# RWKV-7 attention and a quick-GELU MLP in one kernel: where the 64-bit words of the fifth weight piece are staged

## The chip, the cores and the metric

The kernel runs on one core of a Trainium2 chip. The metric is the device time of one execution, in microseconds (us); lower is better. A core has a matrix engine (PE, also called TensorE; its weight loads are listed as PEld), a vector engine (DVE), a scalar engine (ACT), a general engine (POOL), and a queue engine (SP) that issues the DMAs. Each of them takes its instructions strictly in the order in which the program lists them.

## The reference, cut to what matters

```python
def _attn_ref(r, k, v, w, a, b):            # each [4, 8, 768, 40]
    state = np.zeros((B, H, D, D), dtype=np.float32)
    for t in range(S):
        y[:, :, t] = np.einsum('bhd,bhde->bhe', rt, state)
        Sa = np.einsum('bhde,bhe->bhd', state, at)
        state_decay = state * wt[:, :, None, :] - np.einsum('bhd,bhe->bhde', Sa, bt)
        state = state_decay + np.einsum('bhd,bhe->bhde', vt, kt)
    return y

def _moe_ref(x, w_in, w_out):               # x [3072, 320]
    h = x @ w_in                            # w_in [320, 2048]
    g = h * (1.0 / (1.0 + np.exp(-1.702 * h)))
    return g @ w_out                        # w_out [2048, 320]
```

The y of the attention, with its heads laid side by side, is the x of the MLP. The two weight matrices come as 64-bit floats; everything else is 32-bit.

## The kernel before, in words

The sequence of 768 steps is cut into 12 *chunks* of 64. A *unit* is one chunk for two of the four batches, so there are 24 units, numbered i = 2c + p for chunk c and half p. Within a unit the recurrence is turned into matrix products. `decay` makes running products of w; `prep` scales a, b and k by them and forms score matrices; `inverse` inverts a triangular matrix by five doubling levels (the `ps_level` products), in a plain form for the first four units (`PLAIN = 4`, with the tile `PT`) and in another form after them; `solve` applies the inverse (`ps_X`), forms y and the new state (`ps_y`), and writes x, the transposed y. x goes out to DRAM (`part_with`, L911) and comes back in the layout that the MLP needs (`get_back`, L915), into the tile `xT`, of which there are three copies, one for each of three consecutive chunks. Each unit fills one half of its chunk's copy.

`mlp(c)` then does chunk c: products `ps_up` with `w_in`, the activation on ACT (L936), products `ps_down` with `w_out`, and the output store (L959). The down product runs over p and over eight parts m; part m = 0, 1 needs the first piece of `w_out`, 2, 3 the second, and so on.

The weights are loaded once, in eight pieces: 0 to 3 are `w_in`, 4 to 7 are `w_out`. A piece is 1280 64-bit numbers per partition, 1.31 MB. [...]`weight(n, ...)` loads the raw words somewhere (L436), and five steps make 32-bit floats of them in their final place in the tile `w_sb`: L416 on ACT, and L420, L424 and L425, L428 and L432 on DVE. The raw words of a piece take the space of two finished pieces. They lie in one of the following places:

- a half of the tile `extra`, which has room for two pieces of words; this document calls the halves a and b;
- a place inside `w_sb` that a later piece will fill. Piece 1 lies in the place of pieces 4 and 5, piece 2 in that of 6 and 7.

`before` lists the earlier pieces whose words lay at the same spot; the DMA waits until they are finished. `there` lists the pieces whose words still lie where this piece's result goes; L416 waits for those. So pieces 4 and 5 can't be converted before piece 1 is finished, and 6 and 7 not before piece 2. In the kernel before, the list of spots is

```python
raws = [-4, 4, 6, -2, -4, -2, -4, -2]       # -4: half a of extra, -2: half b, 4 and 6: in w_sb
```

The order of all work is made by `Plan`. Every step is a task with a rank, a set of engines that may do it with their assumed durations, and what it reads and writes. `order` simulates the engines: when one comes free, it takes the ready task of lowest rank. `paced` repeats this a few times and spreads the MLP's tasks of a chunk over the time until the next chunk is ready. The instructions are then issued in that order, and each engine waits in it, for its semaphores, at run time. The pieces' ranks are 14, 16, 20, 24, 35, 37, 39, 41; unit i has ranks around 10 i, so piece 4 stands between the work of units 3 and 4. The MLP has ranks from 10000, so it fills whatever the units leave free.

Of the kernel before, what the change touches and what calls it, by code (L numbers as in the profile page):

```python
# [21 lines left out]
INT64 = mybir.dt.int64  # L22
# [203 lines left out]
def rwkv7_gelu_quick(ctx: ExitStack, tc: tile.TileContext, time_d, v_d, w_d, wc_d, ak_d, b_d, rv_d, w_in, w_out, out):  # L226
    nc = tc.nc
    H, D, S = 8, 40, out.shape[0] // 4
    DM = H * D
# [3 lines left out]
    PIECE = w_in.shape[2]  # L233
    NF = w_in.shape[0] * PIECE // DM
    NM = NF // 2
    NK = DM // 64
# [18 lines left out]
    plan = Plan(dict(logw=3, wc=3, G=1, wch=3, wz=2, time=2, ak=2, b=2, rv=2, FT=3, GT=1, kh=2, bh=2, zr=2, rz=2,  # L255
                     A=1, B=1, RV=2, E0=2, W0=2, P21=2, PT=2, W=2, E=2, ES=2, EX=2, T=2, Tc=1, QT=1, zraw=2, zT=1, M=2, x=1, xT=3, g=4, ob=1), 4)
    tiles, psums, drams = {}, {}, {}

    def single(name, shape):
        return const.tile(shape, FP32, tag=name, name=name)  # L260

    def buf(name, n, shape, dt=FP32):

        if (name, n) not in tiles:
            s = n % plan.slots[name]
            tiles[name, n] = work.tile(shape, dt, tag=f"{name}{s}", name=name)
        return tiles[name, n]
# [20 lines left out]
    def act(n):  # L288
        return {"ACT": 210.0 + 0.76 * n}
# [39 lines left out]
    for p in HALF:  # L329
        q = slice(p.start, p.start + MID)  # L330
# [61 lines left out]
    w_sb = single("w_sb", [128, NK * NM * 128 + NF * DM])  # L392
    w_in_sb = w_sb[:, :NK * NM * 128].rearrange("p (m k f) -> p m k f", m=NM, k=NK)
    w_out_sb = w_sb[:, NK * NM * 128:]

    extra = single("extra", [128, 4 * PIECE])


    most, least = (float(np.array(x, np.uint32).view(np.float32)) for x in (0x0FEFFFFF, 0x9FEFFFFF))


    raws = [-4, 4, 6, -2, -4, -2, -4, -2]

    def weight(n, rank, src):
        at = raws[n]
        raw = lambda: (w_sb[:, at * PIECE:(at + 2) * PIECE] if at > 0 else extra[:, (at + 4) * PIECE:(at + 6) * PIECE]).bitcast(INT64)

        scale = lambda: w_sb[:, n * PIECE:(n + 1) * PIECE].bitcast(INT32)

        before = [("weight", m) for m in range(n) if raws[m] == at]  # L410
        there = [("weight", m) for m in range(n) if raws[m] in (n, n - 1)]
        word = lambda dt, w: raw().bitcast(dt).rearrange("p (n two) -> p n two", two=2)[:, :, w]

        def rebased(t):

            nc.scalar.activation(scale().bitcast(FP32), word(FP32, 1), ACT.Prelu, scale=2.0 ** -112, alpha=2.0 ** 32)  # L416

        def bounded(t):

            nc.vector.tensor_scalar(scale().bitcast(FP32), scale().bitcast(FP32), least, most, ALU.max, ALU.min)  # L420

        def exponent(t):

            nc.vector.tensor_scalar(word(INT32, 1), scale(), 3, -2 ** 23, ALU.logical_shift_left, ALU.bitwise_and)  # L424
            nc.vector.tensor_single_scalar(scale(), scale(), 3, op=ALU.logical_shift_left)  # L425

        def fraction(t):
            nc.vector.scalar_tensor_tensor(word(FP32, 1), in0=word(UINT32, 0), scalar=2.0 ** -52, in1=word(FP32, 1),  # L428
                                           op0=ALU.mult, op1=ALU.mult)

        def joined(t):
            nc.vector.tensor_add(scale().bitcast(FP32), scale().bitcast(FP32), word(FP32, 1))  # L432

        one, two = 170.0 + 0.48 * PIECE, 150.0 + 1.05 * PIECE
        T = lambda *names: [(name, n) for name in names]
        plan.add(rank, {"SP": 350.0}, lambda t: nc.sync.dma_start(raw(), src), reads=before, writes=T("wt"), size=128 * PIECE * 8)  # L436
        plan.add(rank, act(PIECE), rebased, reads=T("wt") + there, writes=T("rebased"))
        plan.add(rank, {"DVE": one, "sbuf": True}, bounded, reads=T("rebased"), writes=T("bounded"))
        plan.add(rank, {"DVE": 2 * one, "sbuf": True}, exponent, reads=T("bounded"), writes=T("exponent"))
        plan.add(rank, {"DVE": two, "sbuf": True}, fraction, reads=T("exponent"), writes=T("fraction"))  # L440
        plan.add(rank, {"DVE": two, "sbuf": True}, joined, reads=T("fraction"), writes=T("weight"))

    def weights():
        for n in range(len(raws)):
            weight(n, RANKS[n], w_in[n] if n < NQ else w_out[n - NQ])
# [116 lines left out]
    at = lambda tiles, n: tiles[n % len(tiles)]  # L562
# [1 line left out]
    both = lambda i: zr_of(i)[:, :8 * 104].rearrange("p (j n) -> p j n", n=104)  # L564
    zraw_of = lambda i: buf("zraw", i, [128, 8, D])
    M_of = lambda i: buf("M", i, [128, 8, 104])
    xT_of = lambda c: buf("xT", c, [128, 2, NK, 128])
    kh_of, bh_of = lambda i: kh_t[i % 2], lambda i: bh_t[i % 2]
    zT_of = lambda i: zT_t[i % plan.slots["zT"]]

# [216 lines left out]
    def solve(i):  # L787
        c, p = divmod(i, 2)
        R = 20 * (i // 2) + 5 * (i % 2)
        T = lambda *names: [(n, i) for n in names]  # L790
        ahT = lambda: ak_of(i)[:, 0]

        if c > 0:
            plan.add(R, {"DVE": 490.0, "sbuf": True}, lambda t: nc.vector.tensor_mul(
                both(i)[:, :, 64:], zraw_of(i - 2), wz_of(i).unsqueeze(2).to_broadcast([128, 8, D])),
                     reads=[("zraw", i - 2), ("wz", i)], writes=T("zr"))
# [12 lines left out]
            def read_state(t):  # L809

                ps, rT = psum(t, "ps_rz"), rv_of(i)[:, 0]
                for u, b in product(BITS, BITS):
                    for f, e in QUARTERS:
# [5 lines left out]
                     reads=T("zT"), writes=T("rz"), pair=("rz", i))  # L819
# [94 lines left out]
            for h in HALF:  # L914
                nc.sync.dma_start(xT_of(c)[h, p].rearrange("q k n -> q (k n)"), drams[i].rearrange("(q k) n -> q (k n)", q=64))  # L915
        plan.add(-50, {"SP": 700.0}, part_with, reads=T("x"), writes=T("xd"), size=DM * 512)
        plan.add(-50, {"SP": 700.0}, get_back, reads=T("xd"), writes=[("xT", c), ("xs", (c, p))], size=2 * DM * 512)


    g_of = lambda n: buf("g", n, [128, 2, 2, 256])  # L920
# [60 lines left out]
    for i in range(NU):  # L981
        decay(i)
        if i + 3 < NU:
            load_w(i + 3)
        if i + 2 < NU:
            logarithm(i + 2)
        if i >= 2:
            load(i)
        prep(i)
        inverse(i)  # L990
        solve(i)
        if i % 2:
            mlp(i // 2)
# [88 lines left out]
```

## Time and profile before

| | us |
|---|---|
| median of 3 runs | 727.67 (726.9 to 730.33) |
| the profiled execution's own time | 732.38 |
| its span, first to last instruction | 730.7 |
| PE busy in the span | 679.2 (93%) |
| PEld busy | 557.8 (76%) |
| DVE busy | 426.6 (58%) |
| ACT busy | 352.8 (48%) |
| POOL busy | 211.1 (29%) |

The profile is of one execution, and the times of single instructions come from it. Busy times of engines overlap. The strip shows the busy share of 40 equal slices of the span in tenths; a row of a timeline gives start, duration, engine, source line, operation and tiles, and in brackets how long the engine stood idle before it and what released it. All matrix products have the line L275, so they are told apart by their tiles. Rows with SPq are DMAs being issued; the transfer itself goes on afterwards.

### The profile page before, as it was taken

Reading aid. Unit: us, or ns where it says so; the run is one execution under the profiler, and the core shown is the slowest. Engines: PE = TensorE matmul, PEld = TensorE weight load, DVE = VectorE, ACT = ScalarE, POOL = GpSimd, SP = SyncE. Lnnn points to the kernel's source line nnn. Section 1 sums busy time; section 2 is a strip of 40 time slices with the busy share of each in tenths; the row PEclk is TensorE's granted clock in tenths of the full one; section 3 lists DMA queues with packets and bytes.
Section 4 is the critical chain, followed back from the end, with each engine's and each line's share of the span. In section 5 each row is a group of like instructions: output and inputs, shape, how many; then the busy total and the mean of one; then the engine's idle time right before and its main releaser. Section 6 shows DMA issues by size and latency. Waiting matters only on the chain.

```text
span 730.7 us, 43534 instructions
## 1 busy us (share of the span) xinstructions
PE 679.2 (93%) x20256; PEld 557.8 (76%) x20256; DVE 426.6 (58%) x747; ACT 352.8 (48%) x672; POOL 211.1 (29%) x281
## 2 busy tenths in 40 slices
PE   4575998998999999999999999999999999999997
PEld 4565876686778788888878888879889778867564
DVE  6569798965665656656664655647566666431000
ACT  4465755557445745535636444544536345341120
POOL 7015133522322532333431441331342431200000
PEclk9869999999999999999999999999999999999999
DMA  7952553431422441331340341331341230111000
GB/s 220 346 177 85 173 179 117 123 108 44 127 76 73 118 125 41 117 103 57 100 139 28 104 140 40 109 100 58 100 120 38 79 93 6 40 48 31 15 6 20
DMA packets 31860, 69.81 MB, mean 96 GB/s; under 512 B 5056, under 2 KB 14272, under 8 KB 30656
## 3 DMA queue, kind: packets, MB, share of 16 engines
q1 hardware_dynamic: 31680, 67.03, 29.9%
q8 instruction: 159, 2.61, 1.4%
q14 instruction: 21, 0.17, 0.1%
HBM read 59.15 MB, written 7.86 MB: 92 GB/s over the span
## 4 chain that ended last, share of the span: by engine, by line
PE 83%; DVE 5%; issue 4%; ACT 4%; POOL 2%; DMA 2%; SPq 0%; POOLq 0%; ACTq 0%; DVEq 0%
PE ps_down L275 27%; PE ps_up L275 27%; PE ps_level L275 8%; PE ps_B L275 5%; PE ps_y L275 4%; PE ps_X L275 3%; PE ps_Q L275 2%; PE ps_T L275 1%; PE ps_rz L275 1%; PE ps_A L275 1%; PE ps_N L275 1%; PE ps_zT L275 1%; PE ps_RV L275 1%; DVE w_sb L432 1%; DMA rv<-in_rv 1%
## 5 line engine op out<-in xcount | busy, mean ns | idle before, releaser
L275 PE MATMUL ps_up<-xT,w_sb 64*64 64x256 f32 x3840 | 256.5, 380 | 4.6 <-issue 3.2
L275 PE MATMUL ps_down<-w_sb,g 64*64 64x320 f32 x3072 | 240.1, 431 | 2.4 <-DVE w_sb L432 1.9
L275 PEld LDWEIGHTS ps_up<-xT,w_sb 64*64 64x64 f32 x3840 | 160.4, 134 | 33.9 <-issue 6.7
L275 PEld LDWEIGHTS ps_down<-w_sb,g 64*64 64x64 f32 x3072 | 126.6, 133 | 49.3 <-DVE w_sb L432 2.2
L936 ACT ACTIVATE g<-ps_up 128x1024 f32<-128x1024 f32 x48 | 49.2, 1024 | 48.8 <-PE ps_up L275 48.6
L585 POOL TENSOR_TENSOR kh<-time,G 128x320 f32<-128x320 f32 x24 | 21.8, 909 | 168.1 <-PE ps_y L275 89.9
L664 ACT ACTIVATE EX<-ES,quads 128x256 f32<-128x256 f32 x102 | 46.2, 501 | 47.3 <-DVE ES L659 46.9
L275 PEld LDWEIGHTS ps_level<-W,EX 64*64 64x64 f32 x2560 | 57.0, 134 | 11.2 <-issue 2.3
L708 ACT COPY W<-ps_level 128x512 f32<-128x512 f32 x56 | 32.8, 585 | 60.0 <-PE ps_level L275 58.3
L839 ACT COPY B<-ps_B 128x416 f32<-128x416 f32 x44 | 22.3, 506 | 73.1 <-PE ps_B L275 73.1
L275 PE MATMUL ps_level<-W,EX 64*64 64x64 f32 (+1 forms) x2560 | 56.9, 219 | 0.5 <-ACT EX L664 0.4
L710 DVE TENSOR_TENSOR E<-two,ps_level 128x256 f32<-128x256 f32 x80 | 33.3, 416 | 40.3 <-ACT W L708 39.9
L275 PE MATMUL ps_level<-PT,EX 64*64 64x64 f32 (+2 forms) x1280 | 35.5, 246 | 14.5 <-DVE EX L680 6.8
L275 PEld LDWEIGHTS ps_level<-PT,EX 64*64 64x64 f32 x1280 | 32.8, 146 | 20.6 <-issue 9.4
L962 DVE TENSOR_TENSOR ob<-ob,ps_down 128x320 f32<-128x320 f32 x24 | 11.7, 487 | 62.9 <-ACT ob L960 62.6
L901 POOL TENSOR_TENSOR x<-zr,FT 128x128 f32<-128x128 f32 x84 | 44.4, 557 | 0.4 <-POOL bh L585 0.4
L659 DVE STREAM_TRANSPOSE ES<-E 128x256 f32<-128x256 f32 x80 | 35.6, 445 | 4.3
L275 PE MATMUL ps_y<-RV,kh 64*64 64x104 f32 x768 | 36.0, 250 | 0.9 <-DVE M L855 0.9
L275 PE MATMUL ps_y<-M,bh 64*64 64x104 f32 x768 | 36.1, 249 | 0.2 <-issue 0.2
L577 POOL TENSOR_TENSOR ak<-ak,FT 128x512 f32<-128x512 f32 x22 | 28.6, 1299 | 26.5 <-ACT FT L539 9.7
L855 DVE TENSOR_TENSOR M<-ps_X,later 128x832 f32<-128x832 f32 x24 | 24.6, 1023 | 19.8 <-PE ps_X L275 19.8
L666 POOL TENSOR_TENSOR EX<-ES,quads 128x512 f32<-128x512 f32 x19 | 26.7, 1404 | 23.6 <-DVE ES L659 16.7
(138 smaller groups left out, 1144.4 us busy)
## 6 DMA issues: line engine op xcount, KB each, us to landing
ak<-in_ak SPq DMA_DIRECT2D x48, 160.0 KB
time<-in_time SPq DMA_DIRECT2D x24, 320.0 KB
rv<-in_rv SPq DMA_DIRECT2D x48, 160.0 KB
xT<-x_dram SPq DMA_DIRECT2D x48, 160.0 KB
wc<-in_wc SPq DMA_DIRECT2D x20, 264.0 KB
extra<-in_w_out SPq DMA_DIRECT2D x4, 1280.0 KB
logw<-in_w SPq DMA_DIRECT2D x24, 160.0 KB
b<-in_b SPq DMA_DIRECT2D x48, 80.0 KB
```

The costliest lines, as they stand in the source:

```text
L275: nc.tensor.matmul(o, lhsT, rhs, start=start, stop=True, skip_group_check=True)
L577: plan.add(R, {"DVE": 690.0, "POOL": 1270.0, "sbuf": True}, lambda t: of(t.engine).tensor_mul(ahT(), ahT(), FT_of(i)), reads=T("ak", "FT") ...
L585: plan.add(R + 4, {"POOL": 870.0, "DVE": 490.0, "sbuf": True}, lambda t, n=n, dst=dst: of(t.engine).tensor_mul(dst(i)[:, :, :D], by_head(t ...
L659: plan.add(rank, dve(256), lambda t: nc.vector.transpose(ES(n), source(t)), writes=[key("ES", n, 6)], **reads)
L664: nc.scalar.activation(dst[:, :, h], ES(n), ACT.Copy, scale=quads[:, h, :1])
L666: of(t.engine).tensor_mul(dst, ES(n).unsqueeze(2).to_broadcast([128, 8, 2, 32]), quads.unsqueeze(1).to_broadcast([128, 8, 2, 32]))
L708: plan.add(rank, any2(512), lambda t: copy(t.engine)(tiles_of(W(n + 1)), blocks(psum(t, ""), 64)), writes=[key("W", n + 1, 5)], pair=pair)
L710: plan.add(rank, dve(256), lambda t: nc.vector.tensor_sub(tiles_of(E(n + 1)), every(two32, [128, 2, 4, 32]), blocks(psum(t, ""), 64)[:, :, ...
L839: plan.add(R, any2(416), lambda t: copy(t.engine)(dst(), psum(t, "")[:, :, :208]), writes=[("Bv", i)] if x and c > 0 else T("B"), pair=(na ...
L855: plan.add(R + 1, dve(832), lambda t: nc.vector.tensor_tensor(M_of(i).rearrange("p (j b) n -> p b j n", b=2), psum(t, "")[:, :, :416].rear ...
L901: of(t.engine).tensor_mul(x[:, b ^ u, b], both(i)[:, at, :64], FT_of(i)[:, at])
L936: plan.add(-45, act(1024), lambda t: nc.scalar.activation(g_of(c * NQ + q).rearrange("p m r n -> p r m n"), psum(t, "").rearrange("p r (m ...
```

## The change

The raw words of piece 4 no longer lie in half a of `extra`. They lie in the second and third copy of `xT`, which are together exactly as large as the words of one piece. For that, the three copies of `xT` become one tile, `xT_all`, of the same total size. The pieces after the fifth change halves: 5 and 7 lie in a, 6 in b. The x of chunks 1 and 2, the first to use those two copies, is fetched back only once piece 4 is finished. Ranks, costs and the conversion steps are as before; `PLAIN` is 4 in both kernels.

| piece | 0 | 1 | 2 | 3 | 4 | 5 | 6 | 7 |
|---|---|---|---|---|---|---|---|---|
| words before | a | w_sb 4, 5 | w_sb 6, 7 | b | a | b | a | b |
| DMA waits for piece | - | - | - | - | 0 | 3 | 4 (and 0) | 5 (and 3) |
| words after | a | w_sb 4, 5 | w_sb 6, 7 | b | xT 1, 2 | a | b | a |
| DMA waits for piece | - | - | - | - | - | 0 | 3 | 5 (and 0) |

```diff
     extra = single("extra", [128, 4 * PIECE])
+    xT_all = single("xT_all", [128, plan.slots["xT"], 2 * NK * 128])
...
-    raws = [-4, 4, 6, -2, -4, -2, -4, -2]
+    spots = {"a": (extra, 0), "b": (extra, 2), "w4": (w_sb, 4), "w6": (w_sb, 6)}
+    raws = ["a", "w4", "w6", "b", "x", "a", "b", "a"]
 
     def weight(n, rank, src):
         at = raws[n]
-        raw = lambda: (w_sb[:, at * PIECE:(at + 2) * PIECE] if at > 0 else extra[:, (at + 4) * PIECE:(at + 6) * PIECE]).bitcast(INT64)
+        def raw():
+            if at == "x":
+                return xT_all[:, 1:].rearrange("p s n -> p (s n)").bitcast(INT64)
+            tile, k = spots[at]
+            return tile[:, k * PIECE:(k + 2) * PIECE].bitcast(INT64)
...
         before = [("weight", m) for m in range(n) if raws[m] == at]
-        there = [("weight", m) for m in range(n) if raws[m] in (n, n - 1)]
+        there = [("weight", m) for m in range(n) if raws[m] in (f"w{n}", f"w{n - 1}")]
...
-    xT_of = lambda c: buf("xT", c, [128, 2, NK, 128])
+    xT_of = lambda c: xT_all[:, c % 3].rearrange("p (q k n) -> p q k n", q=2, n=128)
...
-        plan.add(-50, {"SP": 700.0}, get_back, reads=T("xd"), writes=[("xT", c), ("xs", (c, p))], size=2 * DM * 512)
+        plan.add(-50, {"SP": 700.0}, get_back, reads=T("xd") + ([("weight", raws.index("x"))] if c in (1, 2) else []), writes=[("xT", c), ("xs", (c, p))], size=2 * DM * 512)
```

## The prediction

> **What bounds the kernel now.** The strip of 40 slices comes first, to find the stage that a change in weight loading can touch.
>
> ```profile
> PE   4575998998999999999999999999999999999997
> DMA  7952553431422441331340341331341230111000
> ```
>
> Each digit is 18.3 us. After the tenth slice TensorE is full, and nothing that is ready sooner can help it there; all that can be won is in the first ten slices. I then cut those at the events around the weights (busy time per engine by stage):
>
> ```profile
> 20.00:50.00 30.00, 17.99 (x492) 16.46 (x493) 18.49 (x24) 15.46 (x31) 1.47 (x2) 0.68 0.84 294
> 50.00:75.00 25.00, 15.85 (x708) 14.34 (x700) 22.80 (x31) 14.18 (x37) 11.41 (x11) 0.97 0.25 76
> 80.60:107.60 27.00, 25.55 (x770) 23.49 (x766) 21.42 (x28) 17.50 (x26) 7.78 (x8) 1.00 0.48 164
> 107.60:131.70 24.10, 19.27 (x689) 16.59 (x682) 21.83 (x29) 14.21 (x28) 9.34 (x7) 0.93 0.37 123
> 180.00:730.70 550.70, 540.42 (x15836) 438.43 (x15827) 290.35 (x550) 252.20 (x470) 148.41 (x183) 1.00 0.26 75
> ```
>
> The columns are window, length, busy PE, PEld, DVE, ACT, POOL, clock, DMA share, GB/s. PE idles 4.83 us in 107.6 to 131.7, and its clock is below full; it idles 10.3 us in the whole 550 us after 180. In 50 to 75 DVE is the bound (22.8 of 25.0); in 20 to 50 none is, and the DMA engines are at 0.84. What ends the idle time of 107.6 to 131.7 is in PE's timeline (start, length, idle before, releaser):
>
> ```profile
> 114.17 1.31 PE L275 MATMUL ps_down<-w_sb,g 64*64 64x320 f32 x16 [0.56 <-DVE w_sb L432]
> ...
> 121.66 0.69 PE L275 MATMUL ps_level<-PT,EX 64*64 64x64 f32 x32 [0.49 <-POOL EX L666]
> 123.60 1.66 PE L275 MATMUL ps_X<-B,T 64*64 64x104 f32 x32 [1.24 <-DVE T L781]
> 125.05 0.91 PE L275 MATMUL ps_B<-RV,A 64*64 64x104 f32 x16
> ...
> 131.69 1.31 PE L275 MATMUL ps_down<-w_sb,g 64*64 64x320 f32 x16 [1.35 <-DVE w_sb L432]
> ```
>
> Two parts of the first down product wait for L432, the last step of converting a weight piece. Between the down parts of 116.45 and 131.69 there is no MLP work, so PE is left with the short steps of units 3 and 4, whose gaps stay open. Why the last piece (number 7) is that late is in the timelines of SP, ACT and DVE:
>
> ```profile
> 77.90 0.33 SPq L436 DMA_DIRECT2D extra<-in_w_out  x1
> ```
>
> ```profile
> 103.98 1.46 ACT L416 ACTIVATE w_sb<-extra 128x1280 f32<-128x1280 f32 x1 [1.82 <-DMA extra<-in_w_out]
> 113.91 1.42 ACT L416 ACTIVATE w_sb<-extra 128x1280 f32<-128x1280 f32 x1 [0.49 <-DMA extra<-in_w_out]
> ```
>
> ```profile
> 94.55 2.02 DVE L432 TENSOR_TENSOR w_sb<-w_sb,extra 128x1280 f32<-128x1280 f32 x1
> 104.32 1.50 DVE L432 TENSOR_TENSOR w_sb<-w_sb,extra 128x1280 f32<-128x1280 f32 x1
> 111.52 2.60 DVE L432 TENSOR_TENSOR w_sb<-w_sb,extra 128x1280 f32<-128x1280 f32 x1
> 129.54 2.10 DVE L432 TENSOR_TENSOR w_sb<-w_sb,extra 128x1280 f32<-128x1280 f32 x1
> ```
>
> These four L432 end pieces 4 to 7. The pieces' DMAs are issued at 41.88, 77.90, 97.33 and 107.45, each right after the piece that held its half of `extra` is finished (0 at 39.2, 3 at 77.87, 4 at 96.57, 5 at 105.8). ACT then waits for the DMA twice. A chain of buffers sets the last two pieces, not DVE's speed alone.
>
> **What the Trainium skill says.** (1) "DMA: Bandwidth & Descriptors", Where 436 GB/s comes from: about 358 GB/s of HBM per core bind. The trace agrees: 359 GB/s in 20 to 30 us at DMA share 0.97. (2) "Runtime: NRT & Kernel Launch", Instruction fetch mechanics: instructions come by DMA in blocks of 256, mostly hidden. Here only partly: PE has idle pieces of 3.21, 2.98 and 2.01 us marked "issue" at 20.0, 27.3 and 35.6 us, while the DMA engines are full. (3) "TensorE: Matmul & The Clock Gate", What's actually happening: the clock is halved after an idle window. In the trace it is 0.83 in 120 to 130, and X takes 1.66 us there against 0.92 at 150.14. (4) "SBUF — State Buffer", Who interferes with whom: DVE and POOL lock a shared port, DMA does not touch it. The L432 of 111.52 takes 2.60 us beside POOL's L582, the quiet ones 1.49; so where the words lie costs nothing.
>
> **The change, part by part.** Nothing is computed more or less: eight word DMAs, eight L416, 32 DVE steps, the same xT DMAs.
>
> *Piece 4* loses its wait for piece 0. In rank order its DMA falls behind piece 3's (27.81), so about 28 to 33 instead of 41.88. Its L416 was at 58.54, because the place of its result held piece 1's words until 58.4; that stays, and so does its conversion at 80.6 to 96.6 (DVE is full to 80). Gain: nothing.
>
> *Piece 5* now waits for piece 0 instead of 3, so its DMA goes out near 42 in place of 77.90. *Piece 6* waits for 3: 77.9 in place of 97.33. *Piece 7* waits for 5. A piece takes DVE 0.79 + 0.82 + 0.83 + 1.45 + 1.50 = 5.4 us, and DVE idles 27.0 - 21.42 = 5.6 us in 80.6 to 107.6 (the largest hole, 2.92, at 81.4). So about one piece more fits there: piece 5 ends near 101 (105.8 less the holes of 3.8 before 92, and a little back), piece 6 near 110, and piece 7 takes what piece 6 took from DMA to last step, 114.1 - 97.3 = 16.8 us: near 118 in place of 131.6.
>
> *PE.* The down parts that waited until 131.69 can run from 118. Eleven parts of 1.1 to 1.3 us then lie beside the holes of 115 to 131: at most 4.83 us of idle time, and with fewer holes the half clock goes, X's 0.74 and 2 x 0.35 of the B products, 1.4 us. Together 6.3 at most. A part is longer than most holes, so some will overhang into the chain of unit 3: I take three quarters, 4.8.
>
> *Will the gap only move to 131 to 147?* Chunk 1's up products start at 147.08, when the down parts end. To take them sooner, x of unit 3 must be sooner. It can be: L882, which begins the copies from unit 3's y, waits behind the 2.10 us L432 of 129.54, and POOL's last x ends at 134.81, while SP issues its DMA only at 137.09, behind the output store of the late down product. 2.1 + 2.3 = 4.4 us come free, about what is needed.
>
> *Cost in the start-up.* Piece 4's 1.31 MB move ahead and piece 5's take their place, so the DMA engines have 1.31 MB / 358 GB/s = 3.7 us more to do before 50 (an estimate from (1)). Loads of unit 3 that stand behind it on SP are needed by DVE and POOL only from 78 on, 30 us later. But PE's fetches share the engines: 8.2 us of stall came with 637 instructions in 20 to 40, about 3.3 us per block of 256; 3.7 us longer congestion at 355 instructions per 10 us is half a block, 1.7 us, partly under DVE's work. Low end 0 (fetched ahead), high end 4 (one block in full and a late unit 1). I take 0.5.
>
> *The new wait.* The second-half DMAs of x (L915) of chunks 1 and 2 wait for piece 4. It ended at 96.57, the first such DMA is issued at 106.27: covered by 9.7 us. If piece 4 were later than that, SP's loads behind would stand too, piece 7's words among them.
>
> *A new order.* Due times changed, so the planner lays out all later work anew. No view shows that. Bound: 3 us either way, from what the present order leaves idle on PE between 131.7 and 180 (0.3 in the rest of the first MLP, 3.8 after 147.1): a new order can hardly save more than most of that, and I allow as much for a loss. I take 0.
>
> Sum: -4.8 + 0.5 = -4.3 us. The profiled execution took 732.38 us (span 730.7 and 1.7 around), 4.7 above the median, so against the median of 727.67: **723.4 us**, -0.6%.
>
> **Rivals.** *A, the forecast* (0.50): 718 to 726. *B, the gap moves* (0.28): down parts fill 118 to 131, but x of unit 3 comes no sooner, and PE idles before 147 instead. For it: unit 4's levels follow each other by 4 to 5 us and can't fill. Against it: the 4.4 us above. Only the clock's 1.4 is won: 726.3, 724 to 729. *C, slower* (0.14): the earlier words lengthen the fetch stalls of 28 to 52, unit 1's x comes late, and the first up product (75.11) with it, in the place where DVE has no slack. One block is 3.3 us, two 6.6, and the new order may cost 3: past 79.4 for that first up product the gain is gone; with two blocks and half the gain 727.7 + 6.6 - 2.4 = 731.9. *D, it does not do what it says* (0.08): the planner puts the converting steps by rank where they were, piece 7 stays at 130: 727.7.
>
> **How the numbers follow.** About 0.5% (3.6 us) is what a measurement can tell from no change. Faster than 724.0: three quarters of A, a third of B, and a share for a lucky order, 0.53. Slower than 731.3: most of C, a little of D, 0.13. Between: 0.34. The range takes A's low end less the order's luck, and C's value without its tail: 715 to 731.5.
>
> **What would show it.** Right: the L436 of `w_out` at about 30, 42, 78 and 100; the last L432 ending before 120; no ps_down released by L432; PE in 107 to 132 above 22.5 of 24.1 at clock 1.00; the first chunk 1 up product near 143. Wrong: "issue" idle of PE above 10 us in 20 to 52 and the first up product after 77 (C); up products still near 147 with idle before them (B); L915 waiting for L432.

## The result, and the profile after

The changed kernel takes 722.26 us (median of 16 runs, 718.19 to 728.50), the kernel before 730.83 in the same series: **ratio 0.9898, 95% interval 0.987 to 0.9926**. Ratios are estimated from the fast runs of a series and are not the quotient of the two medians, which is 0.9883 here. On the 727.67 us of the prediction the ratio means 7.4 us less, where 4.3 was forecast. The profiled execution took 728.5 us with a span of 726.7, the longest of the 16; "after_again" below gives a second one.

First the strip of the changed kernel:

```profile
PE   4566997999999999999999999999999989999997
DMA  7963542332251341351450440441340230110000
```

and the same stages as before (window, length, then busy PE, PEld, DVE, ACT, POOL, clock, DMA share, GB/s):

```profile
80.60:107.60 27.00, 26.37 (x732) 23.04 (x728) 22.88 (x29) 15.36 (x23) 9.49 (x9) 1.00 0.45 135
107.60:131.70 24.10, 18.16 (x570) 13.73 (x564) 20.69 (x27) 13.83 (x28) 5.89 (x5) 0.86 0.28 96
147.10:180.00 32.90, 32.90 (x1072) 32.49 (x1067) 20.03 (x38) 20.91 (x39) 9.04 (x11) 1.00 0.27 79
```

The stage in which the gain was forecast, 107.6 to 131.7, is worse: PE idles 5.94 us there instead of 4.83, at a lower clock. The gain is one stage on: 147.1 to 180 is full. The kernel before lost 3.8 us in it:

```profile
147.10:180.00 32.90, 29.10 (x928) 24.20 (x923) 19.54 (x37) 21.55 (x35) 9.00 (x11) 1.00 0.26 77
```

The pieces show why the forecast stage didn't move. SP's timeline has the four DMAs of pieces 4 to 7, and DVE's timeline the four L438 (L432 before) that end these pieces:

```profile
31.74 0.33 SPq L442 DMA_DIRECT2D xT_all<-in_w_out  x1
...
43.76 0.33 SPq L442 DMA_DIRECT2D extra<-in_w_out  x1
...
81.13 0.55 SPq L442 DMA_DIRECT2D extra<-in_w_out  x1
...
106.48 0.35 SPq L442 DMA_DIRECT2D extra<-in_w_out  x1
```

```profile
95.76 1.47 DVE L438 TENSOR_TENSOR w_sb<-w_sb,xT_all 128x1280 f32<-128x1280 f32 x1
103.83 1.51 DVE L438 TENSOR_TENSOR w_sb<-w_sb,extra 128x1280 f32<-128x1280 f32 x1
117.50 1.74 DVE L438 TENSOR_TENSOR w_sb<-w_sb,extra 128x1280 f32<-128x1280 f32 x1
128.81 1.49 DVE L438 TENSOR_TENSOR w_sb<-w_sb,extra 128x1280 f32<-128x1280 f32 x1
```

The words come 10, 34 and 16 us earlier for pieces 4, 5 and 6, and 1 us for piece 7. The finished pieces don't follow: 97.2, 105.3, 119.2 and 130.3, against 96.6, 105.8, 114.1 and 131.6. Piece 6 shows the delay in ACT's and DVE's timelines: its words are asked for at 81.13, its ACT step follows at 94.36, and its first DVE step only at 108.01.

```profile
94.36 1.42 ACT L422 ACTIVATE w_sb<-extra 128x1280 f32<-128x1280 f32 x1
...
108.01 0.80 DVE L426 TENSOR_SCALAR w_sb<-w_sb 128x1280 f32<-128x1280 f32 x1
```

PE's down parts wait for L438 as they did before (start, length, idle before, releaser):

```profile
119.30 4.54 PE L275 MATMUL ps_down<-w_sb,g 64*64 64x320 f32 x32 [2.04 <-DVE w_sb L438]
...
130.36 1.31 PE L275 MATMUL ps_down<-w_sb,g 64*64 64x320 f32 x16 [0.44 <-DVE w_sb L438]
```

What differs is the order of everything. The planner saw other ready times, and laid out all five engines' lists anew. So the theories to be told apart are **W**: the words come earlier, and that brings the gain; and **O**: it is the new order alone.

### The profile page after: what moved, and what is told of

It reads as the page before. It is cut to its first block, busy times and chain, and to the rows that moved or that the text cites. A ratio compares the mean times of both kernels' runs of the same rounds, so it can differ in the third digit from the quotient of the medians.

```text
span 726.7 us, 43527 instructions
## 1 busy us (share of the span) xinstructions
PE 677.6 (93%) x20256; PEld 572.5 (79%) x20256; DVE 430.0 (59%) x739; ACT 356.8 (49%) x705; POOL 187.9 (26%) x260
## 4 chain that ended last, share of the span: by engine, by line
PE 83%; DVE 5%; issue 3%; ACT 3%; DMA 3%; POOL 2%; SPq 1%; POOLq 0%; DVEq 0%; ACTq 0%
PE ps_down L275 28%; PE ps_up L275 26%; PE ps_level L275 8%; PE ps_y L275 5%; PE ps_B L275 4%; PE ps_X L275 2%; DMA ak<-in_ak 2%; PE ps_Q L275 2%; PE ps_N L275 1%; PE ps_T L275 1%; PE ps_rz L275 1%; PE ps_A L275 1%; PE ps_RV L275 1%; PE ps_zT L275 1%; PE ps_cum L275 1%
## 5 line engine op out<-in xcount | busy, mean ns | idle before, releaser
L275 PE MATMUL ps_up<-xT_all,w_sb 64*64 64x256 f32 x3840 | 249.1, 378 | 2.6 <-ACT g L942 1.5
L275 PE MATMUL ps_down<-w_sb,g 64*64 64x320 f32 x3072 | 244.4, 434 | 3.1 <-DVE w_sb L438 2.5
L275 PEld LDWEIGHTS ps_up<-xT_all,w_sb 64*64 64x64 f32 x3840 | 160.6, 133 | 26.7 <-ACT g L942 1.8
L275 PEld LDWEIGHTS ps_down<-w_sb,g 64*64 64x64 f32 x3072 | 136.2, 134 | 45.3 <-issue 3.1
L670 ACT ACTIVATE EX<-ES,quads 128x256 f32<-128x256 f32 x116 | 52.6, 501 | 49.7 <-DVE ES L665 49.3
L714 ACT COPY W<-ps_level 128x512 f32<-128x512 f32 x51 | 29.8, 585 | 44.0 <-PE ps_level L275 43.9
L968 DVE TENSOR_TENSOR ob<-ob,ps_down 128x320 f32<-128x320 f32 x24 | 11.6, 484 | 59.4 <-ACT ob L966 59.1
L275 PEld LDWEIGHTS ps_level<-PT,EX 64*64 64x64 f32 x1280 | 34.3, 152 | 15.2 <-DVE EX L686 7.0
L907 POOL TENSOR_TENSOR x<-zr,FT 128x128 f32<-128x128 f32 x84 | 42.8, 539 | 10.4 <-ACT zr L899 10.2
L845 ACT COPY B<-ps_B 128x416 f32<-128x416 f32 x36 | 18.2, 506 | 44.1 <-PE ps_B L275 43.6
L665 DVE STREAM_TRANSPOSE ES<-E 128x256 f32<-128x256 f32 x80 | 35.6, 445 | 3.9
L275 PEld LDWEIGHTS ps_y<-RV,kh 64*64 64x64 f32 x768 | 30.1, 134 | 6.4 <-DVE M L861 2.4
```

What stands on the lines that cost most here:

```text
L275: nc.tensor.matmul(o, lhsT, rhs, start=start, stop=True, skip_group_check=True)
L665: plan.add(rank, dve(256), lambda t: nc.vector.transpose(ES(n), source(t)), writes=[key("ES", n, 6)], **reads)
L670: nc.scalar.activation(dst[:, :, h], ES(n), ACT.Copy, scale=quads[:, h, :1])
L714: plan.add(rank, any2(512), lambda t: copy(t.engine)(tiles_of(W(n + 1)), blocks(psum(t, ""), 64)), writes=[key("W", n + 1, 5)], pair=pair)
L845: plan.add(R, any2(416), lambda t: copy(t.engine)(dst(), psum(t, "")[:, :, :208]), writes=[("Bv", i)] if x and c > 0 else T("B"), pair=(na ...
L907: of(t.engine).tensor_mul(x[:, b ^ u, b], both(i)[:, at, :64], FT_of(i)[:, at])
```

## The experiments

**Buffers and order, each without the other.** The planner may be given one kernel's waits and the instructions another's places. "new_bufs_old_order" is the changed kernel with this edit, in which `words` says where the words lie and `raws` what the planner is told:

```diff
-    raws = ["a", "w4", "w6", "b", "x", "a", "b", "a"]
+    words = ["a", "w4", "w6", "b", "x", "a", "b", "a"]
+    raws = ["a", "w4", "w6", "b", "a", "b", "a", "b"]
...
-            if at == "x":
+            if words[n] == "x":
...
-        plan.add(-50, {"SP": 700.0}, get_back, reads=T("xd") + ([("weight", raws.index("x"))] if c in (1, 2) else []), writes=[("xT", c), ("xs", (c, p))], size=2 * DM * 512)
+        plan.add(-50, {"SP": 700.0}, get_back, reads=T("xd"), writes=[("xT", c), ("xs", (c, p))], size=2 * DM * 512)
```

> The words lie where the change puts them (piece 4 in xT, 5 in a, 6 in b, 7 in a), but every engine keeps the order of the kernel before: the plan is made with the old waits of the pieces and without the new wait of x. At run time only the waits for buffers differ. Theory W (earlier words bring the gain): the DMA of the last piece still stands in its old place in SP's order, but piece 6 no longer waits for piece 4 and piece 7 finds its half free; a part of the gain shows, 1 to 4 us faster than before. Theory O (the gain is the order that the planner lays out anew): the same as before within 1 us, ratio 0.999 to 1.001.

Measured: 732.81 us, ratio **1.0004** (0.9973 to 1.0034). The buffers without the order bring nothing. This run alone does not test early words, though: SP keeps the old order too, and it issues the four DMAs at 39.23, 74.00, 97.33 and 106.84, against 41.88, 77.90, 97.33 and 107.45 before. It shows that the new places by themselves neither gain nor cost.

"old_bufs_new_order" exchanges the two lists, drops the new wait of x, and moves five tasks in the finished order (the DMAs of pieces 4 to 6 and the ACT steps of 5 and 6):

```diff
+    words = ["a", "w4", "w6", "b", "a", "b", "a", "b"]
     raws = ["a", "w4", "w6", "b", "x", "a", "b", "a"]
...
+    for n, m in ((4, 0), (5, 3), (6, 4)):
+        if tasks.index(words_of(n)) < tasks.index(step(m, "joined")):
+            after(words_of(n), step(m, "joined"))
+    for n in (5, 6):
+        if tasks.index(step(n, "rebased")) < tasks.index(words_of(n)):
+            t = step(n, "rebased")
+            tasks.remove(t)
+            tasks.insert(tasks.index(step(n, "bounded")), t)
```

> The opposite: the words lie as in the kernel before, and the compute steps keep the order of the changed kernel; only the word DMAs of pieces 4, 5 and 6 are put behind the end of the piece that held their half (0, 3 and 4), and the ACT step of pieces 5 and 6 just ahead of their first DVE step. So the words are as late as before, in the new order. Theory W: the gain is gone, ratio 0.997 to 1.003, with DVE or ACT waiting for the words. Theory O: as fast as the changed kernel within 2 us, ratio 0.988 to 0.993.

Measured: 724.69 us, ratio **0.9898** (0.9856 to 0.9941), as the changed kernel. The order without the new places brings all of it, within the interval, and theory W falls. The words are as late as before: the DMAs are at 41.56, 77.26, 94.47 and 107.75. The following rows are the last two DMAs in SP's timeline, and the steps that end pieces 6 and 7 in DVE's. Counted from the first up product (75.62 in this run), these pieces are finished after 42.8 and 52.9 us, against 40.8 and 51.9, and 40.6 and 51.6, in the two profiles of the changed kernel: the late words cost the pieces 1 to 2 us, and that doesn't show in the time.

```profile
94.47 0.33 SPq L443 DMA_DIRECT2D extra<-in_w_out  x1
...
107.75 0.35 SPq L443 DMA_DIRECT2D extra<-in_w_out  x1
```

```profile
116.71 1.75 DVE L439 TENSOR_TENSOR w_sb<-w_sb,extra 128x1280 f32<-128x1280 f32 x1
...
127.04 1.49 DVE L439 TENSOR_TENSOR w_sb<-w_sb,extra 128x1280 f32<-128x1280 f32 x1
```

**Piece 4 alone.** `raws = ["a", "w4", "w6", "b", "x", "b", "a", "b"]` in the changed kernel.

> Piece 4 in xT as in the change, but pieces 5 and 7 in b and 6 in a, so that piece 5 waits for piece 3 as before. PE, DVE and POOL get exactly the order of the changed kernel; ACT's and SP's differ in the places of the steps of pieces 5 and 6 alone. Theory W: piece 5 comes 36 us later than in the change, so a good part of the gain goes, ratio 0.993 to 1.000. Theory O: as the changed kernel, ratio 0.987 to 0.992.

Measured: 724.15 us, ratio 0.9902 (0.987 to 0.9935). Piece 5's early words are worth nothing that shows here either. (Piece 6's words come early in their place: the DMA at 45.19 is piece 6's, the one at 79.52 piece 5's.)

**The changed kernel again.**

> The changed kernel once more, for a second profile, since its first was 6 us slower than the median of its runs while that of before was 1.5 slower. Both theories: ratio 0.987 to 0.993; the profile should show what the first one lost near 113 to 124, where PE was at half its clock: there 3 to 5 us less.

Measured: 723.90 us, ratio 0.9879 (0.9822 to 0.9937). The loss that I had expected near 113 to 124 is in both profiles: PE is busy for 19.1 of the 25 us from 107 to 132 in each. They differ in the start-up, with the first up product at 78.42 us there and at 74.54 here. But the spans, 726.7 and 725.6, differ by 1.1 us only, so most of that lead is lost again later, and it is open why the first profile was 6 us above the median. The stage 147 to 180 is full again, with the same order:

```profile
147.00:180.00 33.00, 33.00 (x1090) 30.31 (x1084) 18.98 (x36) 19.27 (x35) 8.66 (x10) 1.00 0.26 77
```

**Where in the order the time is.** To compare kernels whose orders differ, I took a measure of lost time: the time elapsed, less the matmuls done so far times the spacing that each form has where PE is undisturbed (a `ps_up` 54 ns, since 16 take 1.09 us and 40 take 2.38; a `ps_down` 67.5; 104 columns 22; 96 columns 21; 64 columns 14; and so on). Lost time up to a moment, in us:

| kernel | 75 | 132 | 147 | 180 | 250 | end |
|---|---|---|---|---|---|---|
| before | 46.1 | 58.3 | 58.9 | 63.9 | 67.8 | 85.7 |
| new_bufs_old_order | 45.7 | 58.3 | 59.0 | 64.1 | 66.8 | 85.4 |
| after | 46.6 | 60.0 | 60.6 | 60.8 | 62.0 | 81.7 |
| after_again | 44.1 | 55.8 | 56.2 | 56.4 | 57.9 | 80.6 |
| old_bufs_new_order | 44.6 | 58.2 | 59.2 | 59.4 | 61.2 | 78.1 |
| piece4_only | 44.7 | 58.1 | 58.6 | 58.6 | 60.4 | 79.4 |

To 147 the two orders stand alike (58.9 and 59.0 against a mean of 58.7). In 147 to 180 the old order loses 5.0 and 5.1 us, the new one 0 to 0.2. In 180 to 250 it is 3.9 and 2.7 against 1.2 to 1.8, and from there on nothing systematic.

The orders differ everywhere; two of their differences in 147 to 180 were tried as the cause. One is on ACT. The exps of a unit (L536 to L543) begin by loading a table that serves exps and logs; at 140.50 one such load is enough for all rows up to L487. In the old order, the activation L936 stands between the exps of unit 7 and the exp and log work behind them (L550, L486), and each of the four loads a table:

```profile
160.46 1.28 ACT L536 ACT_TABLE_LOAD   x1
...
163.14 1.28 ACT L936 ACT_TABLE_LOAD   x1
...
165.48 1.28 ACT L550 ACT_TABLE_LOAD   x1
...
167.23 1.28 ACT L486 ACT_TABLE_LOAD   x1
```

ACT has 7 table loads in 140 to 180, in the new order 3. The other is on PE: chunk 1's down parts lie between its up products in the new order and behind them in the old one (busy PE with `ps_down` in this stage, before and after_again; the columns are window, length, PE, PEld, DVE, ACT, clock, DMA share, GB/s):

```profile
147.00:180.00 33.00, 1.26 (x16) 0.61 (x16) 0.84 (x2) 0.00 (x0) 1.00 0.26 77
```

```profile
147.00:180.00 33.00, 7.89 (x96) 4.34 (x96) 0.00 (x0) 0.00 (x0) 1.00 0.26 77
```

**One task moved, in both kernels.** 735 is the task of unit 7's exps (the expectations count the units one too low) and 393 the activation of the second quarter of chunk 1; this is the edit in before, and in after the exps go ahead of 393 (`+ 0`):

```diff
     tasks = plan.paced(list(paces.values()), ROUNDS, WINDOW, SHARE)
+    exps, gelu = (next(t for t in tasks if t.n == n) for n in (735, 393))
+    tasks.remove(exps)
+    tasks.insert(tasks.index(gelu) + 1, exps)
```

> The kernel before, with one task moved in the finished order: ACT's exps of unit 6 (L536 to L543) stand just behind the activation (L936) of the second quarter of chunk 1, instead of just ahead of it. Nothing else moves. In the kernel before, that activation comes between the exps and the rest of the unit's exp and log work, and ACT loads its function table three times more; PE idles 3.8 us in 147 to 180. Theory T (the table loads there are what PE waits for, and most of the gain of the new order): 3 to 4 table loads in 140 to 180 instead of 7, PE idle there below 1.5 us, ratio 0.993 to 0.997. Theory S (the order differs everywhere and the gain is spread): within 0.997 to 1.002.

Measured: 730.60 us, ratio 0.9979 (0.9954 to 1.0003): no difference that is clear, although 3 table loads remain in 140 to 180. Theory T's figure for the loads was right and its figure for PE was not; its range for the ratio is missed by little and reached by the interval. PE's timeline shows what is late next, and the stage's row how long PE is busy:

```profile
164.73 0.69 PE L275 MATMUL ps_level<-W,EX 64*64 64x64 f32 x32 [1.23 <-POOL EX L666]
```

```profile
147.00:180.00 33.00, 30.01 (x976) 25.06 (x972) 18.42 (x35) 18.76 (x34) 9.06 (x11) 1.00 0.27 76
```

With the table loads gone, this level waits for POOL, and in the stage PE still idles 3.0 us, where it was 3.8.

> The changed kernel with the same task moved the other way: the exps of unit 6 stand just ahead of the activation of the second quarter of chunk 1, as in the kernel before. Theory T: 6 to 7 table loads in 140 to 180 instead of 3, PE idle there 2 to 4 us, ratio 0.993 to 0.997 where the changed kernel has 0.990. Theory S: as the changed kernel, 0.988 to 0.992.

Measured: 729.39 us, ratio 0.9947 (0.9923 to 0.9972): half of the gain lost or more (the quotient of the medians, 729.39 to 732.31, is 0.9960), with 6 table loads in 140 to 180 and 4.2 us of PE idle time in 147 to 180. That is about as T expected. In PE's timeline the up products wait for the delayed activation:

```profile
164.39 2.59 PE L275 MATMUL ps_up<-xT_all,w_sb 64*64 64x256 f32 x32 [3.14 <-ACT g L942]
```

```profile
147.00:180.00 33.00, 28.80 (x857) 22.77 (x852) 15.47 (x30) 20.29 (x30) 7.84 (x10) 0.95 0.25 74
```

The table loads are only a part of that delay. ACT begins the first of them at 158.75 and the activation at 163.31; in these 4.6 us lie two loads of 1.28 us, the exps, and 0.60 us of waiting for POOL. So the place of the exps is shown to matter here, and the loads by themselves are not. Neither theory holds in both kernels: by S the changed kernel should have stayed at 0.988 to 0.992.

**The down parts moved.** In the changed kernel (416 to 423 are the first down parts of chunk 1, 403 the last up product of its third quarter, 723 B products of unit 6; here too the expectation counts one too low):

```diff
+    def behind(n, o):
+        tasks.remove(task[n])
+        tasks.insert(tasks.index(task[o]) + 1, task[n])
+    behind(416, 403)
+    for n, o in ((417, 723), (418, 417), (419, 418), (420, 419), (421, 420), (422, 421), (423, 422)):
+        behind(n, o)
```

> The changed kernel with eight tasks moved in the finished order: the first eight down parts of chunk 1 no longer lie between its up products. The first goes behind the last up product of the third quarter, where the kernel before had it, and the other seven come in one block behind the B products of unit 5. Nothing else moves. In 147 to 180 the order of the change has 68 to 96 down instructions on PE, that of before 16. Theory F (the down parts between the up products fill the gaps of units 4 and 5): PE idle in 147 to 180 of 1.5 to 4 us, ratio 0.992 to 0.997. Theory N (where they lie is indifferent, the gaps are not there in this order): as the changed kernel, 0.988 to 0.991.

Measured: 729.42 us, ratio 0.9976 (0.9961 to 0.9992). The stage loses 2.9 us again:

```profile
147.00:180.00 33.00, 30.12 (x1016) 24.40 (x1011) 19.55 (x38) 20.03 (x36) 8.65 (x10) 1.00 0.29 87
```

Theory F holds for the idle time. The ratio lies a little above its range, with an interval that reaches into it. The seven late parts now follow as one block from 185.33 on, and PE idles 1.4 us in 180 to 215, against 0.1 and 0.5 in the two profiles of the changed kernel.

> Both moves in the changed kernel: the eight down parts late and the exps of unit 6 ahead of the activation of the second quarter of chunk 1, nine tasks in all. If these two places carry the gain between 147 and 180: PE idle of 4 us or more there, ratio 0.994 to 1.000. If the gain is spread over the whole order: not above 0.994.

Measured: 736.71 us, ratio 1.0076 (1.0052 to 1.01), worse than expected. In the stage the two losses add up: PE idles 7.0 us, where the moves alone gave 4.2 and 2.9. The mean clock is 0.95, as with the exps moved alone:

```profile
147.00:180.00 33.00, 26.03 (x798) 20.08 (x790) 15.95 (x31) 21.25 (x35) 8.11 (x10) 0.95 0.22 63
```

```profile
160.31 3.09 PE L275 MATMUL ps_up<-xT_all,w_sb 64*64 64x256 f32 x32 [4.09 <-ACT g L942]
```

The ratios suggest more than a sum, 1.8% against 0.5% and 0.8%, but each has an interval of 0.2 to 0.3% to either side, so that is barely clear. Nine of 2608 tasks cost 1.8% here, from 0.990 to 1.008. All this shows which places the new order must not lose. It does not show that they make up the gain: repairing one of them in the old order brought nothing clear, and giving that order early down parts was not tried.

**Is the better order what the change brings, or a draw?** The assumed fetch time of the planner is changed by 1.4%, in both kernels, in either direction:

```diff
-    BLOCK, FETCH, BESIDE, AHEAD = 256, 3550.0, 0.4, 300.0
+    BLOCK, FETCH, BESIDE, AHEAD = 256, 3500.0, 0.4, 300.0
```

> The kernel before with one number of the planner changed, the assumed time of an instruction fetch from 3550 to 3500 ns (1.4%): nothing of the computation or the buffers, but the order is laid out anew and differs from the old one as much as that of the change does. Theory L (the new order of the change was a lucky draw among orders that scatter by about 1%): anything from 0.985 to 1.015. Theory D (the earlier words let the planner find better orders as a rule): within 0.996 to 1.004.

> The changed kernel with the same number of the planner changed. Theory L: anything from 0.985 to 1.015, and no nearer to the changed kernel than to the kernel before. Theory D: 0.985 to 0.994, as the changed kernel.

> A third draw of the planner: the kernel before with an assumed instruction fetch of 3600 ns in place of 3550. Theory L (a draw): again anything from 0.985 to 1.015, the draw at 3500 having given 1.008 for the kernel before. Theory D: within 0.996 to 1.004.

> The changed kernel with 3600 ns. At 3550 it stands 0.990 to the kernel before with the same number, at 3500 1.0096 to 1.0083. Theory L: its ratio to the kernel before with 3600 has no settled sign, within 0.985 to 1.015. Theory D: 1% faster than before_fetch_3600.

Measured, as ratios to the kernel before (3550), and the table loads of ACT in the whole execution:

| fetch, ns | waits of before | table loads | waits of after | table loads |
|---|---|---|---|---|
| 3500 | 1.0083 (1.0056 to 1.011) | 51 | 1.0096 (1.0068 to 1.0124) | 49 |
| 3550 | 1 | 43 | 0.9898 (0.987 to 0.9926) | 38 |
| 3600 | 1.0091 (1.0058 to 1.0124) | 55 | 1.0029 (1.0004 to 1.0055) | 45 |

Theory D falls: both kernels leave its ranges at 3500. The changed kernel is no faster than the other one with 3500, 0.6% faster with 3600, 1.0% with 3550. Three pairs can't say whether the new waits help by some tenths of a per cent on the average; that stays open. That orders scatter by 2%, twice the gain, is shown. The order with the fewest table loads is the fastest, but it is not shown that the loads are the cause.

## Why the prediction was right or wrong

The measured time lies in the range and the sign is right, but the mechanism was not, so the hit was luck: the gain came from a term that I had put at 0.

- *The bound, and where a gain could lie*: right in part. Up to the tenth slice there was something to win and behind it little, and most of the gain did come there, but in 147 to 180 and not in 107.6 to 131.7; the table of lost time puts another 1 to 2 us of it behind 180.
- *Piece 4*: right. Its DMA is at 31.74 (28 to 33), its end at 97.2.
- *Pieces 5 to 7*: this is the step of the mechanism that failed. The words of 5 and 6 came as forecast (43.76, and 81.13, right behind the end of piece 3). But I let the DVE steps move into DVE's idle time of 80.6 to 107.6, which shrank only from 5.6 to 4.1 us. DVE works through a list that the planner has filled by rank, and the steps of 5 to 7 stand in it about where they stood: the ends are 105.3, 119.2 and 130.3 instead of 101, 110 and 118. Piece 7 then waits for piece 5 as long as before. On the weights, rival D (0.08) was the right one.
- *PE, 4.8 us*: wrong; the holes that were to close stayed, 5.94 us where there were 4.83.
- *x of unit 3*: did not come sooner by what was forecast. Counted from chunk 0's first up product, which takes the start-up out, its fetch (L921, L915 before) is issued after 64.2 and 63.6 us in the two profiles, after 64.4 before. Chunk 1's first up product does come 3 us sooner, after 69.0 and 68.5 us (147.45 and 143.03) instead of 72.0 (147.08). But by 147 us the new order has lost as much time as the old one on the average (table above), so PE only does its work in another sequence; that the second profile meets the forecast "near 143" owes 0.6 us to its start-up and the rest to the new order.
- *Start-up*: not C. The first up product is at 78.42 and 74.54 in the two profiles of the same kernel, against 75.11 and 74.29 in the old order. The pieces marked "issue" are as large as before within that scatter, so the cost is not settled; 0.5 us is not contradicted. The third of the prediction's stalls, at 35.6, fell in a stretch with a DMA share of 0.67, so the DMA engines were not full then.
- *The new wait*: right. x's first guarded DMA is issued at 102.56, 5.3 us behind piece 4's end; the planned order is the same with the wait and without it.
- *A new order*: the mis-sized term. I took 0 with 3 us either way. The two runs with buffers and order exchanged put the whole of the gain, 7.4 us, into this term, and the three pairs show orders 14 us apart. The range of 715 to 731.5 would have left out three of the other draws (1.0083 to 1.0096 of 727.67 are 733.7 to 734.7).
- *The clock*: the Trainium skill's "TensorE: Matmul & The Clock Gate" says under What's actually happening that the clock is halved after an idle window. That agrees with the stage 147 to 180: the mean clock is 0.95 where PE stands still for 3.14 or 4.09 us in one piece, with the exps moved and with both moves, and 1.00 in the kernel before, where 3.8 us of idle time come in pieces of at most 1.49. Long pieces are not needed everywhere: in 107.6 to 131.7 of the kernel before none is longer than 1.35 us, and the clock was 0.93. The gain of 1.4 us from the clock did not come; it was 0.86 there in both profiles of the changed kernel.
- *The place of the words at no cost*: right, by new_bufs_old_order.

## What to carry to other kernels

Where a greedy planner or scheduler lays out the instruction order, an edit of one buffer is two edits, the buffer and a new order: hold the order fixed and change the buffer, then the reverse, before a cause is named. Draw a few orders by a meaningless change of a planner's constant first, since their scatter (2% here) is what any edit has to beat. An engine that takes instructions in a fixed order does not use an operand that comes early: look for the place of the step in its list, not for idle time near by.

## What the runs showed of the hardware that I had not expected

The same kernel's profiles differ by up to 4 us in the first 80 us (first up product at 78.42 and 74.54), which is half of this change's effect, while their spans differ by 1.1; a single pair of profiles can't place a gain of this size.

The idle time of PE from two disturbances in the same stage added up almost exactly (4.2 and 2.9 us apart, 7.0 together). The clock did not follow the sum of the idle time: in 107.6 to 131.7 the kernel before idled 4.83 us at a mean clock of 0.93, and before_one_moved 4.97 us at 1.00.

One table load on ACT served the exps and logs of a whole group (140.50 in the kernel before). With another activation in between, the same lines and that activation took four loads of 1.28 us each.
